# Lightning attention and FNet mixing: the second pair's first layer in two levels, its weight sums moved, folds and output stores reordered

## The chip, the cores and the metric

The kernel runs on one core of a Trainium2 chip. The metric is the device time of one execution in microseconds; lower is better. "Time before" is the median of three runs.

## The reference

Inputs: q, k, v of shape (4, 8, 768, 64), a decay `lam` per head, and two weight matrices of 512 x 2048 and 2048 x 512. All is fp32. The two stages, cut to what matters:

```python
# stage 1: per head, blocks of 64 rows, a running state of 64x64
intra = (qb @ kb.T * Dmask) @ vb
inter = (qb * lam_pow) @ kv_state
out   = intra + inter
kv_state = lam_block * kv_state + (kb * rev_pow).T @ vb
# bridge: (B, H, S, D) -> x of shape (B, S, 512)
# stage 2
mixed = real(fft(fft(x, axis=1), axis=2))
u  = x + mixed
un = (u - mean(u)) / sqrt(var(u) + 1e-6)      # over the last axis
y  = u + maximum(un @ w_ch1, 0) @ w_ch2
```

## The kernel before, in words

TensorE (PE) does all matrix products in fp32; one fp32 matmul leaves two records in the trace. The 24 row tiles of 128 rows (4 batches `b`, 6 tiles each) are grouped in twos: `ORDER` lists 12 groups, the first four are `PLAIN`, the last eight `LATE`. `HC` is 3, `G` is 2, `DM` 512, `DFF` 2048.

*Front, to about 421 us.* `attn(b)` walks six chunks of 128 rows per batch. `fft_ln(b)` does the Fourier mixing: symmetric parts of x are first folded on VectorE (DVE), so that PE multiplies by small cosine and sine matrices. `fold_a(b)` folds the rows that a gather brings mirrored, `fold_b(b, sets)` the rest, for two blocks of 128 and 65 rows, each with an even set `fe` (named `e`) and an odd set `fo` (named `o`). Per block it issues the two full-row folds (L435, L436), the half-row ones (L438, L439), one ScalarE copy, and then even and odd ones in turn (L479 to L493); the second block follows the first. Then PE makes five pieces, `for i in range(5)` (matmul L525); pieces 0, 1 and 4 read the even sets, 2 and 3 the odd ones. A layer norm follows in `norm`. Groups in `PLAIN` go through the plain perceptron `mlp` (first layer L643, second L657, output additions L668 and L669), woven with the attention of the next batch by a list of due times. The normalised rows of `LATE` groups are stored to DRAM as `utd`, their residual rows as `ud`. `combine_weights` (L708) makes Strassen-like sums of weight blocks: `s2.A` and `s2.B` name seven left and right factors, `PRODUCTS` pairs them.

*Late part, 421 us to the end.* The eight `LATE` groups are four pairs j = 0..3 of 512 rows. Both layers of a pair are 2x2 block products done with seven multiplications instead of eight. One level: `first_layer(j)` runs eight column blocks of seven products of width 256 (L892). Two levels: `deep_first(j, k)` splits each of the seven products again into seven, so it has 49 units of four matmuls of width 128 (L977); `deep_second(j, k)` (L1047, reads L1053 and L1055) is the second layer in two levels. `DEEP = 2` gives pairs 0 and 1 the one-level first layer and pairs 2 and 3 the two-level one.

A two-level product needs four sums of the quarters of its weight block, S1 to S4. Three of them are kept in DRAM (`sd`, `td` for the second layer) and loaded again as `tx` tiles by SyncE (SP) one product ahead (`prepare_w`, `prepare_b`, `load_three`); S3 overwrites quarter A21 of its block. GpSimd (POOL) makes the sums of w2 during `first_layer(0)` (`keep_sums`) and those of w1 during `first_layer(1)` (`keep_sums_w`), with SP storing them; `place_sums_w` then loads the seven S3 into place with SP.

`inputs(j)` combines a pair's activations, which `load_u(j)` fetches in two halves of 512 KB into the single `ur` buffer: in the two-level form eight DVE sums (L805 to L822) and ten GpSimd ones (L828 to L832). For the one-level form they are four DVE sums (L793 to L799). `load_u(j + 1)` is issued by SP at the end of `first_layer(j)`, or after product 6 of `deep_first`.

`in_step` fixes the order of the late part: a list of products, each of seven units; product k issues its units at ticks 7k, 7k + 2, up to 7k + 12, so two neighbouring products alternate, and the inputs of product k + 1 are made one step per tick during product k. `seven(mm, read)` goes through seven units on three PSUM banks X, Y, Z; a unit's result is read (L1055 on DVE, L1053 on ScalarE) before the bank takes the next one. After product 1 and 3 of the second layer GpSimd adds the residual rows (`add_u`, L1061); at 5 and 6 the tiles are stored.

`store(b, T, y, cols)` writes a finished tile. Row tiles T < 3 go by a plain DMA on SP (L630); the others have mirrored rows and go by an indirect DMA on GpSimd (L632). Both write into the one tensor `out`. For the last pair, product 5 ends with one store, and product 6 with three.

In `tc.keep_in_program_order` the program's order is kept for an instruction; others may be placed by the scheduler by its own estimates of time. Both orders follow from the code when it is built.

Of the kernel before, what the change touches and what calls it, by code (L numbers as in the profile page):

```python
# [76 lines left out]
def kernel(  # L77
# [25 lines left out]
    G = 2  # L103
# [138 lines left out]

    xs, xn_, xd = {}, {}, {}
# [47 lines left out]
    def attn_out(b, c, head):  # L291
# [23 lines left out]
        if not last:  # L315
            pu = psum_a([128, HP, D])
            for hp in range(HP):
                for hi in range(2):
                    h = 2 * hp + hi
                    mm(pu[HD[hi], hp, :], lhsT=kd[:, h, :], rhs=vt[:, h, :], start=True, stop=True)  # L320
            if c == 0:
                nc.vector.tensor_copy(s_new, pu)
            else:
                nc.gpsimd.tensor_tensor(s_new, s_old, spow.broadcast_to([128, HP, D]), op=ALU.mult)
                nc.vector.tensor_tensor(s_new, s_new, pu, op=ALU.add)
            if not padded:
                yield 0.9
# [39 lines left out]
        if b not in TURNED:  # L367
            x = xn_[b, c] = new(xp, [C, DM], "x") if c < HC else new(xn, [C, DM], "xn")
            back(oT, x)
            if c == 0:  # L370
                xd[b] = (dram.tile([S - 256, DM], F32, name=f"xa{b}"), dram.tile([257, DM], F32, name=f"xb{b}"))
                nc.scalar.dma_start(xd[b][1][256:257], x[0:1])
            elif not last:
                nc.scalar.dma_start(xd[b][0][(c - 1) * C:c * C], x)
            if c >= NC - 2:
                nc.scalar.dma_start(xd[b][1][(c - NC + 2) * C:(c - NC + 3) * C], x)
            if c == NC - 2 and b - 1 not in LEADS:
                mirror_a(b)
            elif last:
                mirror_b(b)  # L380
            yield 1.7
            return
# [85 lines left out]

    def fold_b(b, sets):
# [30 lines left out]
    def fft_ln(b):  # L500
# [19 lines left out]
        for i in range(5):  # L520
# [106 lines left out]

    def store(b, T, y, cols=slice(0, DM)):
        if T < HC:
            nc.sync.dma_start(out[b, 128 * T:128 * T + 128, cols], y[:, cols])  # L630
        else:
            nc.gpsimd.indirect_dma_start(out=out.rearrange("b s d -> (b s) d"),  # L632
                                         out_offset=row_of(2 + HC * (b + 1) + T - HC),
                                         in_=y[:, :], in_offset=None)
# [98 lines left out]
    s2.sd = []  # L733

    def quarters_w(t):

        return [t[:, k, f:f + FH // 2] for f in (0, FH // 2) for k in range(2)]

    def keep_sums_w(k):

        pin = tc.keep_in_program_order
        A11, A12, A21, A22 = quarters_w(s2.A[PRODUCTS[k][0]])
        S3, S2, S1, S4 = [new(s2.yp, [128, FH // 2], "tx", bufs=6) for _ in range(4)]
        s2.sd.append([dram.tile([128, FH // 2], F32, name=f"sd{k}{i}") for i in range(4)])
        for i, o, x, y, op in ((3, S3, A11, A21, SUB), (1, S2, A22, S3, SUB), (0, S1, S2, A11, ADD), (2, S4, A12, S2, SUB)):
            pin(nc.gpsimd.tensor_tensor(o, x, y, op=op))
            nc.sync.dma_start(s2.sd[k][i], o)
# [29 lines left out]
    DEEP = 2  # L777
# [107 lines left out]
    def first_layer(j):  # L885
# [24 lines left out]
        for i in range(HF):  # L910
# [17 lines left out]
            if j < min(DEEP, 2) and i < len(PRODUCTS):  # L928
# [13 lines left out]
        if j + 1 < PAIRS:  # L942
            load_u(j + 1)
# [7 lines left out]
    def seven(mm, read):  # L951

        X, Y, Z = (bank() for _ in range(3))
        for m, ps, start, where in ((0, X, True, (0, 0, 1)), (1, Y, True, (0, 0, 0)), (2, X, False, (1, 0, 1)),
                                    (3, Z, True, (1, 1, 1)), (4, X, False, (1, 1, 0)), (5, Z, False, (1, 0, 0)),
                                    (6, X, False, (0, 1, 1))):
# [7 lines left out]
    def deep_first(j, k):  # L964
# [25 lines left out]

        yield from seven(mm, read)
# [39 lines left out]
    def deep_second(j, k):  # L1031
# [18 lines left out]
        def read(ps, s, m, first):  # L1050
# [3 lines left out]
            else:  # L1054
                V.tensor_tensor(o, ps[:, 0:HM // 2], o, op=ADD)  # L1055

        yield from seven(mm, read)
# [91 lines left out]
    def late():  # L1149
        for j in range(PAIRS):  # L1150
            if j < DEEP:
                open_pair(j)
                if j == 0:
                    run(inputs(0))
                first_layer(j)
                if j + 1 < DEEP:
                    in_step(second_layer(j) + [(inputs(j + 1), iter(()))])
# [116 lines left out]
```

## Time and profile before

| what | value |
|---|---|
| median of 3 runs | 791.47 us (790.59 to 792.36) |
| the profiled execution | 791.45 us |
| its span on the core | 789.2 us |
| mean TensorE clock granted | 0.997 |
| TensorE busy | 761.4 us, 96% |
| VectorE busy | 586.2 us, 74% |
| GpSimd busy | 198.2 us, 25% |

The span runs from the first to the last recorded event; 2.25 us of the execution lie outside it. Busy time adds up an engine's instructions; an engine can be idle because it waits for another, and only the waits on the chain that ends last lengthen the run. Rows of a timeline give start, length, engine, line, operation, tiles written and read, shapes, and in square brackets the idle time before it with what ended that idle time.

### The profile page before, as it was taken

The numbers are of one execution on the slowest core, as the hardware profiler recorded it, in microseconds if no ns is written. First come the engines' busy times: TensorE is split into PE (matmuls) and PEld (weight loads), VectorE is DVE, ScalarE is ACT, GpSimd is POOL, SyncE is SP. The second block draws the span as 40 slices with busy tenths as digits, with TensorE's granted clock in tenths as the row PEclk, the third lists the DMA queues.
The fourth block names the chain that finished last, engine by engine and source line by source line (L and its number), as shares of the span: only waits on it lengthen the run. The fifth ranks groups of instructions, "written<-read, shape, count | busy, mean of one in ns | idle before, by whom it ended". The sixth has DMA issues, their size and how long they took to land.

```text
span 789.2 us, 14621 instructions
## 1 busy us (share of the span) xinstructions
PE 761.4 (96%) x5616; PEld 646.2 (82%) x5616; DVE 586.2 (74%) x1148; ACT 225.4 (29%) x532; POOL 198.2 (25%) x197
## 2 busy tenths in 40 slices
PE   6989989999999999999999999999999999999996
PEld 5767776858675877858846889988999999999996
DVE  5899889685846382345798998669966699758983
ACT  3765443325531221422101221022211342024300
POOL 3223331011102010211004950289105001220021
PEclk9999999999999999999999999999999999999998
DMA  9978723337843147521343375245944455455442
GB/s 230 266 157 226 197 100 121 93 65 208 224 134 87 54 81 146 135 87 41 72 102 107 149 253 151 89 174 200 350 144 148 148 176 185 130 172 186 127 124 79
DMA packets 152331, 116.80 MB, mean 148 GB/s; under 512 B 113998, under 2 KB 113998, under 8 KB 152262
## 3 DMA queue, kind: packets, MB, share of 16 engines
q1 hardware_dynamic: 147120, 103.39, 46.7%
q0 software_dynamic: 2112, 6.69, 2.5%
q10 hardware_dynamic: 3030, 5.78, 2.0%
q8 instruction: 45, 0.74, 0.4%
q14 instruction: 24, 0.20, 0.1%
HBM read 83.58 MB, written 32.25 MB: 147 GB/s over the span
## 4 chain that ended last, share of the span: by engine, by line
PE 82%; DVE 9%; DMA 4%; issue 2%; ACT 2%; POOL 1%; POOLq 0%; ACTq 0%
PE p L1047 22%; PE p L892 12%; PE p L977 11%; PE pm L657 11%; PE pm L643 10%; PE pa L525 3%; PE pa L341 3%; PE pa L300 3%; DMA x<-xb,ix 2%; PE pa L335 2%; PE pa L276 1%; PE pa L320 1%; PE pa L281 1%; PE pa L357 1%; DVE sc L304 1%
## 5 line engine op out<-in xcount | busy, mean ns | idle before, releaser
L643 PE MATMUL pm<-ut,w 128*128 128x256 f32 x512 | 118.4, 381 | 0.0
L657 PE MATMUL pm<-w,hr 128*128 128x512 f32 x256 | 115.3, 596 | 0.1
L643 PEld LDWEIGHTS pm<-ut,w 128*128 128x128 f32 x512 | 94.5, 190 | 13.6 <-issue 2.1
L657 PEld LDWEIGHTS pm<-w,hr 128*128 128x128 f32 x256 | 46.7, 190 | 50.3 <-issue 48.9
L1061 POOL TENSOR_TENSOR y<-y,u 128x512 f32<-128x512 f32 x12 | 18.9, 1571 | 199.1 <-DVE y L1070 156.7
L1047 PE MATMUL p<-tx,sx 128*128 128x128 f32 x416 | 54.9, 275 | 0.0
L1047 PEld LDWEIGHTS p<-tx,sx 128*128 128x128 f32 x416 | 50.6, 192 | 0.0
L892 PE MATMUL p<-ur,w 128*128 128x256 f32 x192 | 46.7, 379 | 0.0
L272 POOL TENSOR_TENSOR kd<-k,decay 128x512 f32<-128x512 f32 x20 | 22.6, 1129 | 95.4 <-PE pa L320 55.9
L1053 ACT COPY y<-p 128x128 f32<-128x128 f32 x48 | 12.8, 267 | 104.1 <-PE p L1047 103.1
L1055 DVE TENSOR_TENSOR y<-p,y 128x128 f32<-128x128 f32 x92 | 25.6, 286 | 22.5 <-PE p L1047 15.9
L892 PEld LDWEIGHTS p<-ur,w 128*128 128x128 f32 x192 | 36.4, 190 | 5.3 <-issue 0.5
L1047 PE MATMUL p<-w,ha 128*128 128x128 f32 x288 | 37.4, 275 | 0.0
L304 DVE TENSOR_TENSOR sc<-pa,decay 128x512 f32<-128x512 f32 x48 | 31.5, 683 | 7.4 <-PE pa L300 7.2
L300 PEld LDWEIGHTS pa<-qT,kT 64*128 64x128 f32 x384 | 26.1, 193 | 12.8 <-ACT qT L283 7.6
L1047 PEld LDWEIGHTS p<-w,ha 128*128 128x128 f32 x288 | 35.0, 192 | 0.2
L651 ACT ACTIVATE hr<-pm 128x256 f32<-128x256 f32 x44 | 16.7, 385 | 62.5 <-PE pm L643 62.2
L300 PE MATMUL pa<-qT,kT 64*128 64x128 f32 x384 | 30.8, 292 | 3.2 <-ACT qT L283 2.9
L892 PE MATMUL p<-sx,w1s 128*128 128x256 f32 x128 | 32.9, 380 | 0.5 <-DVE sx L795 0.5
L558 POOL TENSOR_SCALAR ve<-mv 128x2 f32<-128x2 f32 x12 | 3.3, 279 | 117.6 <-DVE mv L555 117.6
L341 PE MATMUL pa<-sc,v 128*64 128x128 f32 x384 | 30.6, 283 | 2.0 <-DVE sc L304 1.9
L632 POOL DMA_INDIRECT out_dram<-y,ix x12 | 12.7, 1057 | 77.3 <-DVE y L669 56.0
(234 smaller groups left out, 1734.7 us busy)
## 6 DMA issues: line engine op xcount, KB each, us to landing
tx<-td SPq DMA_DIRECT2D x84, 256.0 KB, 2.8
raw<-in_moe_w_ch_dram SPq DMA_DIRECT2D x32, 512.0 KB, 4.4
tx<-sd SPq DMA_DIRECT2D x42, 256.0 KB, 2.7
sd<-tx SPq DMA_DIRECT2D x28, 256.0 KB, 2.0
k<-in_k_dram SPq DMA_DIRECT2D x24, 256.0 KB, 5.9
q<-in_q_dram SPq DMA_DIRECT2D x24, 256.0 KB, 4.3
v<-in_v_dram SPq DMA_DIRECT2D x24, 256.0 KB, 5.1
td<-tx SPq DMA_DIRECT2D x21, 256.0 KB, 2.0
```

Source lines behind the costliest of these rows:

```text
L272: nc.gpsimd.tensor_tensor(kd, kt, kpow, op=ALU.mult)
L300: mm(pss[hi][:, hp, :], lhsT=kT[HD[hi], hp, :], rhs=qT[HD[hi], hp, :], start=True, stop=True)
L304: nc.vector.tensor_tensor(t, pss[hi], decay[:, hi::2, :], op=ALU.mult)
L341: mm(po[HD[hi], hp, :], lhsT=vt[:, 2 * hp + hi, :], rhs=sc[hi][:, hp, :], start=(c == 0 and hp == 0), stop=(hp == HP - 1), skip_group_chec ...
L525: mm = nc.tensor.matmul(ps[:, n, :], lhsT=piece(a, i, n), rhs=cs[0:rows, a, i in (2, 3), n, :], start=(a == 0), stop=(a == 1))
L643: nc.tensor.matmul(ps, lhsT=w1[:, c, 128 * fc:128 * fc + 128], rhs=ut[:, c, :], start=(c == 0), stop=(c == KO - 1))
L657: nc.tensor.matmul(ps, lhsT=hr[(fc - f0) // 4][:, fc % 4, 128 * i:128 * i + 128], rhs=w2[:, fc, :], start=(fc == f0), stop=(fc == f1 - 1))
L892: nc.tensor.matmul(ps, lhsT=s2.A[a][:, kt, 128 * i:128 * i + 128], rhs=U[b][:, kt, :], start=(first and kt == 0), stop=(kt == 1), skip_gro ...
L977: nc.tensor.matmul(ps[:, 128 * i:128 * i + 128], lhsT=ab[m][0][:, 128 * i:128 * i + 128], rhs=ab[m][1], start=(start and i == 0), stop=Tru ...
L1047: nc.tensor.matmul(ps[:, 0:HM // 2], lhsT=ab[m][0][i], rhs=ab[m][1][:, i, :], start=(start and i == 0), stop=(i == HF // 2 - 1), skip_grou ...
L1055: V.tensor_tensor(o, ps[:, 0:HM // 2], o, op=ADD)
L1061: nc.gpsimd.tensor_tensor(o, y, u, op=ADD)
```

## The change

`DEEP` becomes 1: pair 1 takes the two-level first layer too. The sums of w1 are therefore needed before pair 1 begins. They are made in four places:

- `front_sums`: products 0, 1 and 5, on DVE after the state update of chunk 1 of batch 3, into spare front tiles, stored by GpSimd's queue.
- `sums_of_first`: products 3 and 4, on DVE during the second layer of pair 0, one step after every second read of products 2 to 4, staged in a tile that has the place of `ur`, stored by GpSimd's queue.
- `sums_beside(2)` and `sums_beside(6)`: on GpSimd, at product 5 of the second layer of pair 0 and at the first product of pair 1.
- `place_sums_w` loads three S3 instead of seven; in the other four products S3 is made in place.

`load_u(j + 1)` for pair 1 moves from the end of `first_layer(0)` to after product 4 of the second layer of pair 0. Separately, `folds_apart` replaces `fold_b` for b = 2 and 3: the even folds of both blocks are issued first, then the odd ones; and pieces are made in the order 0, 1, 4, 2, 3 for every b. The output is written through two views declared disjoint, one for SP and one for GpSimd. The last pair's product 6 runs its units in the order 0, 2, 3, 5, 4, 1, 6, and part of its tiles are stored at product 5, the last tile in parts. The core of the diff:

```diff
+    def block_sums(eng, queue, k, t, stage, inside, pin=tc.keep_in_program_order):
+        Q11, Q12, Q21, Q22 = quarters_w(t)
+        d = sums_of[k] = [dram.tile([128, DFF // 4], F32, name=f"sd{k}{i}") for i in range(4)]
+        o = dict(enumerate(stage))
+        if inside:
+            o[3] = Q21
+        for i, x, y, op in ((3, Q11, Q21, ALU.subtract), (1, Q22, 3, ALU.subtract), (0, 1, Q11, ALU.add), (2, Q12, 1, ALU.subtract)):
+            x, y = (o[z] if isinstance(z, int) else z for z in (x, y))
+            pin(eng.tensor_tensor(o[i], x, y, op=op))
+            if i < 3 or not inside:
+                queue.dma_start(d[i], o[i])
+            yield 0.0
+
+    def front_sums():
+        fa, fb = slice(0, DFF // 2), slice(DFF // 2, DFF)
+        for k, a in ((0, w1[:, 0:2, fa]), (1, w1[:, 2:4, fa]), (5, w1[:, 2:4, fb])):
+            third = new(fp, [128, DM + 4], "ds")[:, 0:DM]
+            second = new(np_, [128, DM], "un", bufs=1)
+            first_, fourth = (new(ep, [128, DM], "e") for _ in range(2))
+            yield from block_sums(nc.vector, nc.gpsimd, k, a, (first_, second, fourth, third), False, lambda i: i)
...
-                nc.vector.tensor_tensor(s_new, s_new, pu, op=ALU.add)
+                grown = nc.vector.tensor_tensor(s_new, s_new, pu, op=ALU.add)
...
+            if (b, c) == (B - 1, 1):
+                with tc.issue_after(grown.ins):
+                    run(front_sums())
...
+    def folds_apart(b, sets):
+        tt = nc.vector.tensor_tensor
+        parts = [(eo[b][a], xs[b, a][0:n], xs[b, HC + a][0:n], n) for a, n in enumerate(BLK)]
+        for (e, o), lo, hi, n in parts:
+            tc.keep_in_program_order(tt(e[0:n, 0, 0:DM], lo, hi, op=ALU.add))
+            tt(e[0:n, 0, 1:HM], e[0:n, 0, 1:HM], e[0:n, 0, HM:DM - 1], op=ALU.add)
+            nc.scalar.copy(e[0:n, :, HM:HM + 1], e[0:n, :, DM - 1:DM])
...
+        for (e, o), lo, hi, n in parts:
+            tc.keep_in_program_order(tt(o[0:n, 0, 0:DM], lo, hi, op=ALU.subtract))
...
-            run(fold_b(b, sets))
+            run((folds_apart if b > 1 else fold_b)(b, sets))
...
-        for i in range(5):
+        for i in (0, 1, 4, 2, 3):
...
+    out_low, out_high = dram_disjoint_views(out.rearrange("b s d -> (b s) d"), 2)
...
-            nc.sync.dma_start(out[b, 128 * T:128 * T + 128, cols], y[:, cols])
+            row = S * b + 128 * T
+            nc.sync.dma_start(out_low[row:row + 128, cols], y[:, cols])
         else:
-            nc.gpsimd.indirect_dma_start(out=out.rearrange("b s d -> (b s) d"),
+            nc.gpsimd.indirect_dma_start(out=out_high,
...
-        for k, (a, _) in enumerate(PRODUCTS):
-            nc.sync.dma_start(quarters_w(s2.A[a])[2], s2.sd[k][3])
+        for k in (0, 1, 5):
+            tc.keep_in_program_order(nc.sync.dma_start(quarters_w(s2.A[PRODUCTS[k][0]])[2], s2.sd[k][3]))
+
+    def sums_of_first():
+        ur = new(s2.up, [128, 2, KO, G * 128], "ur").rearrange("p a b c -> p (a b c)")
+        for k in (3, 4):
+            yield from block_sums(V, nc.gpsimd, k, s2.A[PRODUCTS[k][0]], four(ur), True)
+
+    def sums_beside(k):
+        u = [new(s2.yp, [128, G, DM], "u2", bufs=2).rearrange("p s c -> p (s c)") for _ in range(2)]
+        run(block_sums(nc.gpsimd, nc.gpsimd, k, s2.A[PRODUCTS[k][0]], four(*u), True))
...
-    DEEP = 2
+    DEEP = 1
...
-                (keep_sums, keep_sums_w)[j](i)
+                keep_sums(i)
...
-        if j + 1 < PAIRS:
-            load_u(j + 1)
         open_y(j)
...
+        if (j, k) == (DEEP, 0):
+            sums_beside(6)
         yield from seven(mm, read)
...
+            P.reads = P.reads + 1
+            if P.sums and P.reads % 7 in (1, 3, 5):
+                next(P.sums, None)
+        if j < DEEP and k == 2:
+            P.sums = sums_of_first()
+        if j < DEEP and k == 5:
+            sums_beside(2)
-        yield from seven(mm, read)
+        yield from seven(mm, read, (0, 2, 3, 5, 4, 1, 6) if (j, k) == (PAIRS - 1, 6) else range(7))
...
+            if j < DEEP:
+                run(P.sums)
+                load_u(j + 1)
         elif k == 5:
             store(*who[1][1], yt[:, 1, 1])
+            if j == PAIRS - 1:
+                store(*who[1][0], yt[:, 1, 0])
+                store(*who[0][0], yt[:, 0, 0], slice(0, HM))
         else:
             store(*who[0][1], yt[:, 0, 1])
-            store(*who[1][0], yt[:, 1, 0])
-            store(*who[0][0], yt[:, 0, 0])
+            if j == PAIRS - 1:
+                for m in (0, HM // 2):
+                    store(*who[0][0], yt[:, 0, 0], slice(HM + m, HM + m + HM // 2))
```

More of the change, by code (lines that the diff above doesn't have):

```diff
@@ L7 @@
 from concourse import mybir
+from concourse.bass_types import dram_disjoint_views
 from concourse.masks import make_identity
@@ L240, in weights, with quarters_w @@
                 yield 1.0
+    def quarters_w(t):
+        return [t[:, k, f:f + DFF // 4] for f in (0, DFF // 4) for k in range(2)]
+    sums_of = {}
+    def block_sums(eng, queue, k, t, stage, inside, pin=tc.keep_in_program_order):
[17 more added lines that the diff above has]
+            yield from block_sums(nc.vector, nc.gpsimd, k, a, (first_, second, fourth, third), False, lambda i: i)
     xs, xn_, xd = {}, {}, {}
@@ L467, in fold_a @@
             yield from fold_x(b, a, n, 1, eo[b][a][1][0:n, 1, 0:DM], xn_[b, HC + a][0:n])
+    def folds_apart(b, sets):
[5 more added lines that the diff above has]
+            nc.scalar.copy(e[0:n, :, HM:HM + 1], e[0:n, :, DM - 1:DM])
+            am = e[0:n, :, W:2 * W]
+            lo, hi = e[0:n, 0, 0:HM + 1], e[0:n, 1, 0:HM + 1]
+            tt(am[:, 0, 0:HM + 1], lo, hi, op=ALU.add)
+            tt(am[:, 1, 0:HM + 1], lo, hi, op=ALU.subtract)
+            lo, hi = am[:, :, 0:QM], am[:, :, HM:QM:-1]
+            tt(e[0:n, :, 0:QM], lo, hi, op=ALU.add)
+            tt(e[0:n, :, QM:HM], lo, hi, op=ALU.subtract)
+            yield 2.4
+        for (e, o), lo, hi, n in parts:
+            tc.keep_in_program_order(tt(o[0:n, 0, 0:DM], lo, hi, op=ALU.subtract))
+            tt(o[0:n, 0, 1:HM], o[0:n, 0, 1:HM], o[0:n, 0, HM:DM - 1], op=ALU.subtract)
+            bm = o[0:n, :, W:2 * W]
+            lo, hi = o[0:n, 0, 1:HM], o[0:n, 1, 1:HM]
+            tt(bm[:, 0, 1:HM], lo, hi, op=ALU.subtract)
+            tt(bm[:, 1, 1:HM], lo, hi, op=ALU.add)
+            lo, hi = bm[:, :, 1:QM + 1], bm[:, :, HM - 1:QM - 1:-1]
+            tt(o[0:n, :, 0:QM], lo, hi, op=ALU.subtract)
+            tt(o[0:n, :, QM:HM], lo, hi, op=ALU.add)
+            yield 2.4
+            sets.append((e, o))
+        eo.pop(b)
     def fold_b(b, sets):
@@ L731, in keep_sums, with four @@
             nc.sync.dma_start(s2.td[k][i], o)
[L733 to L747, printed above, removed]
-    def place_sums_w():
-        for k, (a, _) in enumerate(PRODUCTS):
-            nc.sync.dma_start(quarters_w(s2.A[a])[2], s2.sd[k][3])
+    s2.sd = sums_of
+    def four(*tiles):
+        return [t[:, i:i + 512] for t in tiles for i in range(0, t.shape[1], 512)]
+    def place_sums_w():
+        for k in (0, 1, 5):
[7 more added lines that the diff above has]
+        run(block_sums(nc.gpsimd, nc.gpsimd, k, s2.A[PRODUCTS[k][0]], four(*u), True))
     def load_u(j, queue=nc.sync):
@@ L927, in first_layer @@
             last = (i, X, Z)
-            if j < min(DEEP, 2) and i < len(PRODUCTS):
+            if i < len(PRODUCTS):
                 if i == 0:
                     tc.keep_in_program_order(nc.gpsimd.tensor_copy(s2.begun, h["a11"][:, 0, 0, 0:1]))
-                (keep_sums, keep_sums_w)[j](i)
+                keep_sums(i)
             if i == HF - 3:
@@ L949, in part_sum, with seven @@
             e.tensor_tensor(o[:, s], x[:, s], y[:, s], op=op)
-    def seven(mm, read):
+    def seven(mm, read, order=range(7)):
         X, Y, Z = (bank() for _ in range(3))
-        for m, ps, start, where in ((0, X, True, (0, 0, 1)), (1, Y, True, (0, 0, 0)), (2, X, False, (1, 0, 1)),
-                                    (3, Z, True, (1, 1, 1)), (4, X, False, (1, 1, 0)), (5, Z, False, (1, 0, 0)),
-                                    (6, X, False, (0, 1, 1))):
+        steps = ((0, X, True, (0, 0, 1)), (1, Y, True, (0, 0, 0)), (2, X, False, (1, 0, 1)),
+                 (3, Z, True, (1, 1, 1)), (4, X, False, (1, 1, 0)), (5, Z, False, (1, 0, 0)),
+                 (6, X, False, (0, 1, 1)))
+        for m, ps, start, where in (steps[i] for i in order):
             if m:
@@ L1055, in read @@
                 V.tensor_tensor(o, ps[:, 0:HM // 2], o, op=ADD)
-        yield from seven(mm, read)
+            P.reads = P.reads + 1
+            if P.sums and P.reads % 7 in (1, 3, 5):
+                next(P.sums, None)
+        if k == 0:
+            P.reads, P.sums = 0, None
+        if j < DEEP and k == 2:
[3 more added lines that the diff above has]
+        yield from seven(mm, read, (0, 2, 3, 5, 4, 1, 6) if (j, k) == (PAIRS - 1, 6) else range(7))
         def add_u(o, y, k, m):
@@ L1086, in deep_second @@
             V.tensor_tensor(y12, y12, T, op=ADD)
+            if j < DEEP:
+                run(P.sums)
+                load_u(j + 1)
         elif k == 5:
             store(*who[1][1], yt[:, 1, 1])
+            if j == PAIRS - 1:
+                store(*who[1][0], yt[:, 1, 0])
+                store(*who[0][0], yt[:, 0, 0], slice(0, HM))
         else:
             store(*who[0][1], yt[:, 0, 1])
-            store(*who[1][0], yt[:, 1, 0])
-            store(*who[0][0], yt[:, 0, 0])
+            if j == PAIRS - 1:
+                for m in (0, HM // 2):
+                    store(*who[0][0], yt[:, 0, 0], slice(HM + m, HM + m + HM // 2))
+            else:
+                store(*who[1][0], yt[:, 1, 0])
+                store(*who[0][0], yt[:, 0, 0])
     def sum_s3(j):
@@ L1149, in late @@
     def late():
[L1150 to L1157, printed above, removed]
+        open_pair(0)
+        run(inputs(0))
+        first_layer(0)
         in_step(second_layer(DEEP - 1) + [w for j in range(DEEP, PAIRS) for w in deep_pair(j)])
```

## The prediction

> **What bounds the kernel now.** I read the page first, then busy time by windows, then the chain of waits, then timelines where the diff bites.
>
> ```profile
> PE 761.4 (96%) x5616; PEld 646.2 (82%) x5616; DVE 586.2 (74%) x1148; ACT 225.4 (29%) x532; POOL 198.2 (25%) x197
> ```
>
> TensorE bounds the span of 789.2 us; 28 us are not its own. The windows (stretch, length, then busy time of each engine) say where:
>
> ```profile
> 262.00:345.00 83.00, 83.00 (x631) 63.87 (x631) 36.71 (x82) 22.30 (x57) 12.70 (x17) 1.00 0.45 102
> 421.00:607.00 186.00, 185.46 (x1240) 173.24 (x1239) 155.87 (x278) 33.15 (x97) 91.93 (x73) 1.00 0.52 176
> 607.00:782.00 175.00, 174.68 (x1565) 174.49 (x1563) 138.71 (x247) 45.61 (x95) 26.28 (x30) 1.00 0.49 151
> ```
>
> From 421 us PE idles under 1 us, so PE work removed there is time gained, and work on VectorE, GpSimd or a queue is free until it makes PE wait. The chain of waits (start, length, what) is PE alone at the end, and closes with an output store:
>
> ```profile
> 696.82 38.41 PE p L977 x344
> 740.59 35.75 PE p L1047 x320
> 776.93 4.39 DMA out_dram<-y,ix
> ```
>
> **The second pair's first layer.** From the PE timeline, one-level and two-level rows:
>
> ```profile
> 553.96 1.03 PE L892 MATMUL p<-sx,w1s 128*128 128x256 f32 x4
> 554.83 1.89 PE L892 MATMUL p<-ur,w 128*128 128x256 f32 x8
> ...
> 610.89 1.06 PE L977 MATMUL p<-sx,tx 128*128 128x128 f32 x8
> 611.79 1.06 PE L977 MATMUL p<-sx,w1s 128*128 128x128 f32 x8
> ```
>
> Matmul ends overlap, so I take start to start. One-level: four records (one product of width 256) in 0.87 and 1.72/2 = 0.86; I use 0.864. Two-level: eight records in about 0.893 (the last units of the run begin at 777.05, 777.95, 778.84 and 779.73, the same spacing). The first layer of pair 1 has 8 blocks × 7 = 56 units, 56 × 0.864 = 48.4 us; afterwards 7 × 7 = 49 units, 49 × 0.893 = 43.8 us. **−4.6 us**, firm, as the other two pairs already run this form in a dense window.
>
> **Early folds (b = 2 and 3).** The PE timeline has one wait in each, for an even fold (L484) of the second block:
>
> ```profile
> 256.04 1.25 PE L525 MATMUL pa<-cs,fe 65*128 65x193 f32 x6 [1.75 <-DVE fe L484]
> ...
> 366.09 1.09 PE L525 MATMUL pa<-cs,fe 65*128 65x193 f32 x5 [0.95 <-DVE fe L484]
> ```
>
> VectorE starts the first block when a gather has landed and alternates even and odd:
>
> ```profile
> 247.97 0.69 DVE L435 TENSOR_TENSOR fe<-x,x 128x512 f32<-128x512 f32 x1 [2.83 <-DMA x<-xb,ix]
> 248.58 0.69 DVE L436 TENSOR_TENSOR fo<-x,x 128x512 f32<-128x512 f32 x1
> ```
>
> The steps are 0.61 for a whole-row operation and 0.34 for a half. Both blocks' evens are 2 × (0.61 + 5 × 0.34) = 4.6 us, so evens end near 252.6, plus about 1 us for a ScalarE copy between two of them: 253.6–254.0, before PE asks at 254.3. Gain 1.75. For b = 3 VectorE can start at 357.8: evens end near 363.0, while in the changed order of PE's instructions the first even piece stands where PE would come at about 362.5. A rest of about 0.5 may stay: gain 0.45. The odd folds end 257–259 and 366–368, and PE, which takes piece 4 ahead of 2 and 3, wants them at about 261 and 369. The changed order of pieces for b = 0 and 1 only permutes PE work: 0 ± 0.2. Does the gain reach the end? Between 345 and 421 VectorE combines weights; it then has 2.0 us idle before L668 at 421.5, which waits on PE, so an earlier PE finds a VectorE that can be about 2 us earlier. **−2.2 us** (−1.0 to −2.7).
>
> **The block sums' new places.** GpSimd lost 28 sums in the pair-1 first layer (PE dense beside them: worth 0). In their stead:
>
> - 12 VectorE sums of 128x512 at 301.7–319 (12 × 0.61 = 7.3 us). VectorE is idle there for 8.33, 3.03, 3.03 and 3.43 us ahead of the reads at 310.0, 313.5, 316.9 and 321.4; PE is at 100%. Every read has at least one spare PSUM buffer. The 12 GpSimd stores at about 1.0 us each (nearest row: L632, 1057 ns mean) hold back one state decay needed at 324 and the kd products at 319.4. Value 0, bounds 0 and +1.5.
> - 8 VectorE sums at 480–500, one at every second read, beside about 6 us of idle time: 4.9 us, lag at most 1.3. PE reaccumulates a bank four units later (3.6 us, 2.7 after the unit itself), so nothing shows: 0.
> - SP's loads `place_sums_w` fall from 7 to 3, its 28 stores go: 0, as SP gated nothing there.
>
> **The reload of `ur`.** This is the new wait. The last of the eight sums leaves VectorE near 497.8; its GpSimd store lands near 501.1; only then may SP issue the two halves of `ur` (all staged in it), which take 5.7 us (the page's issue rows: `ur<-utd` 5.7). SP keeps its queue order, so a `td` load and half 1 stand behind the first half: half 1 lands near 507.6. VectorE's first operation on it is due at 506.8 (the same operation of the next pair, L805, 598.96, minus the 92.2 us period). So it is 0.8 to 1.7 us late. Before, SP issued this load at 470.5, and it cost nothing.
>
> At the same time GpSimd makes four sums and three stores (504–512) beside eight SBUF-to-SBUF operations of VectorE, and it shows what that costs:
>
> ```profile
> 501.70 1.33 DVE L873 TENSOR_TENSOR sx<-sx,ha 128x512 f32<-128x512 f32 x1
> ...
> 503.73 0.99 DVE L875 TENSOR_TENSOR sx<-ha,sx 128x512 f32<-128x512 f32 x1 [0.30 <-PE p L1047]
> 504.64 0.28 DVE L1055 TENSOR_TENSOR y<-p,y 128x128 f32<-128x128 f32 x1
> 504.84 0.68 DVE L793 TENSOR_TENSOR sx<-ur 128x512 f32<-128x512 f32 x1
> ```
>
> Beside a GpSimd operation of 1.27 us the same shape takes 1.33 or 0.99 instead of 0.68: +0.65 or +0.31. Four meetings at up to 0.65 are 2.6 us. The Trainium skill (page "SBUF — State Buffer", section "SBUF: two separate sides") goes further: VectorE with two SBUF inputs and a GpSimd operation that reads SBUF take one port pair as an exclusive lock, and the loser waits for the whole instruction. By that rule a meeting may cost up to 1.27 us, four of them 5.1. The row decides: nothing here lost more than about one GpSimd operation's half, so I take 2.6. Lag 1.3 + 2.6 = 3.9 us; PE feels what exceeds 2.7: **+1.2 us** by the row, +3.7 by the rule. Lower bound 0 (meetings missed), upper bound +4.
>
> The same page warns, in its box on VectorE blocking DMAs, that a GpSimd-queue DMA starves while VectorE runs a two-port mode, which speaks against storing by GpSimd. It names copies and single-input operations, not two-input sums; the indirect stores here land in 2.7–2.9 us beside a busy VectorE, so I charge nothing.
>
> **The tail.** The end of the old run: PE's last unit starts 780.63, VectorE's last read is at 781.72, GpSimd issues an indirect store at 782.09, and SP's two stores come 3 us later, because both write `out` and SP waits for the indirect landing:
>
> ```profile
> 782.09 0.97 POOL L632 DMA_INDIRECT out_dram<-y,ix  x1 [4.16 <-DVE y L1055]
> 784.91 0.81 SPq L630 DMA_DIRECT2D out_dram<-y  x2
> ...
> SPq L630 <- DMA out_dram<-y,ix: 14.4, 2, 10.9
> ```
>
> (the last line is of the waits of SP). The span closes at 789.2. Two views remove that wait, and half of the last pair's output leaves at product 5. What is late next: the indirect store of `who[0][1]`. It is ready near 780.2 but stands behind the previous indirect store (issued 776.93, 4.39 us, so 781.3): issue 781.4, landing 784.2–785.8. SP's two last pieces issue at 782.1–782.5 and land near 784.7. Add the 1.2 us that lay between last landing (788.0) and end: 786.0–787.0, **−2.8 us** (−1.5 to −3.4).
>
> **The sum.** −4.6 −2.2 −2.8 +1.2 = −8.4. The profiled execution took 791.45 (span 789.2 and 2.25 around it), 0.02 from the median 791.47. 791.45 − 8.4 = **783.1 us**, span about 780.8.
>
> **Rivals.**
> - *No new stall* (0.22): GpSimd's sums fall between VectorE's operations and `ur` is on time. −9.6: 781.9; with the best fold and tail bounds 780.3.
> - *Smaller gains, larger stall* (0.20): tail −1.5, folds −1.0, stall +2 to +3.7: −5.1 to −3.4, so 786.3–788.1. The indirect landing of 4.39 us speaks for the tail part; the page's lock rule for the stall.
> - *The `ur` chain becomes the bound* (0.07, slower or no gain): sum, GpSimd store, SP reload, VectorE and PE in series, with SP's queue in order behind the wait. Hidden while half 1 lands by about 509; after that each microsecond is one of PE. To cancel the 9.6 us gained it must land near 519–520, i.e. a GpSimd store must be 11 us late. For it: GpSimd's queue stands ahead of SP's, and a wait there delays three more things. Against: the six stores stand ahead of GpSimd's three long additions at 500, and stores land in under 3 us. At 13 us late: about 793.
> - *It does not do what it says*: excluded for the order of instructions. In the built program SP's last stores wait on no GpSimd DMA, and even folds stand first.
>
> **How the numbers follow.** My forecast (783.1) has 0.51, the rivals 0.22, 0.20 and 0.07. Measurement tells apart about 0.2% (1.6 us). The range 780.3 to 787.5 takes in the forecast, the first rival and most of the second. Slower by over 0.2% gets 0.05, within it 0.03, faster 0.92.
>
> **What would show it.** Right: PE's first-layer stretch of pair 1 is 43.8 us of L977-like units; no PE gap before the even pieces of b = 2, under 0.6 for b = 3; SP's last stores no longer wait on an indirect landing; PE gaps of about 1 us in total near 505–515. Wrong: PE gaps over 4 us behind the `ur` reload, SP's `ur` issue after 505, fold gaps unchanged, or the last indirect store landing after 786.

## The result, and the profile after

| | before | after |
|---|---|---|
| median | 790.92 us (14 executions) | 787.33 us (14 executions) |
| ratio | | 0.9949, interval 0.993 to 0.9969 |
| profiled execution | 791.45 us, span 789.2 | 784.18 us, span 782.3 |

The kernel became faster by 4.0 us by the ratio (0.51% of 791) and by 3.6 by the medians, where 8.4 were forecast; 787.33 lies just inside the range given. Two later sets of executions of the unaltered changed kernel had ratios of 0.994 (0.9917 to 0.9962) and 0.9931 (0.9904 to 0.9957). Over all sets, executions of either kernel spread over 8 us and more. Two traces of the changed kernel, 8 us apart, differ almost only ahead of 130 us, where little of the change lies (the order of the fold pieces of b = 0). So below I compare stretches that begin there.

The marks are lines of the chain of waits (start, length, what): the first fold product of b = 1 (the expectations below call it that of b = 0), the start of the long first-layer stretch of pair 0 on the chain, and the last long second-layer stretch. Before (the third mark, 740.59, is in the prediction):

```profile
130.96 2.63 PE pa L525 x16
...
423.72 45.13 PE p L892 x208
```

After:

```profile
129.91 2.62 PE pa L588 x16
...
421.64 45.15 PE p L959 x208
...
736.35 41.11 PE p L1115 x368
```

| stretch | before | after | difference |
|---|---|---|---|
| front (first mark to second) | 292.76 | 291.73 | −1.03 |
| late (second to third) | 316.87 | 314.71 | −2.16 |
| tail (third to end of span) | 48.61 | 45.95 | −2.66 |
| sum | 658.24 | 652.39 | −5.85 |

Another 1.05 us of the two profiled spans' difference lies before the first mark, and 0.37 outside the span (2.25 before, 1.88 after). Each column is one trace. In later traces of the same code the front and the late stretch differ from these by up to 0.5 us, so smaller differences say nothing.

TensorE is still the bound (first part of the page), and the windows show where it has gaps now (same columns as in the prediction):

```profile
PE 756.1 (97%) x5784; PEld 646.6 (83%) x5784; DVE 603.0 (77%) x1159; ACT 231.9 (30%) x532; POOL 190.5 (24%) x210
```

```profile
262.00:345.00 83.00, 82.15 (x630) 61.75 (x630) 46.41 (x93) 21.34 (x56) 19.99 (x30) 1.00 0.55 144
421.00:607.00 186.00, 183.53 (x1437) 177.40 (x1437) 160.57 (x276) 40.82 (x99) 82.44 (x80) 1.00 0.56 184
607.00:775.00 168.00, 168.00 (x1507) 168.00 (x1506) 136.70 (x241) 44.19 (x93) 22.29 (x24) 1.00 0.50 151
```

The first window had 83.00 of 83.00 before, the second 185.46 of 186.00. The PE timeline names the gaps; the wait for b = 2 (1.75 us) is gone, that for b = 3 is not, and three are new (one of 0.94 at 147 us is the same in both kernels):

```profile
312.86 4.15 PE L709 MATMUL pm<-ut,w 128*128 128x256 f32 x18 [0.85 <-DVE hr L715]
...
361.52 1.25 PE L588 MATMUL pa<-cs,fe 65*128 65x193 f32 x6 [0.97 <-DVE fe L515]
...
508.60 1.16 PE L1115 MATMUL p<-w2s,sx 128*128 128x128 f32 x8 [0.72 <-DVE y L1123]
...
512.75 1.16 PE L1115 MATMUL p<-tx,sx 128*128 128x128 f32 x8 [1.21 <-DVE y L1123]
```

All are waits for VectorE. At 508 to 513 its timeline shows both suspects at once, operations that last two to three times 0.68 us and a wait for the reload of `ur`:

```profile
502.91 1.42 DVE L1162 TENSOR_TENSOR y<-y 128x512 f32<-128x512 f32 x1
504.25 0.28 DVE L1123 TENSOR_TENSOR y<-p,y 128x128 f32<-128x128 f32 x1
504.45 1.56 DVE L1163 TENSOR_TENSOR y<-y,t 128x512 f32<-128x512 f32 x1
506.12 0.29 DVE L1123 TENSOR_TENSOR y<-p,y 128x128 f32<-128x128 f32 x1
507.65 0.69 DVE L872 TENSOR_TENSOR ur<-ur 128x512 f32<-128x512 f32 x1 [1.24 <-DMA ur<-utd]
508.26 0.28 DVE L1123 TENSOR_TENSOR y<-p,y 128x128 f32<-128x128 f32 x1
508.46 1.88 DVE L875 TENSOR_TENSOR sx<-ur 128x512 f32<-128x512 f32 x1
...
510.47 1.23 DVE L877 TENSOR_TENSOR ur<-ur 128x512 f32<-128x512 f32 x1
```

What the two PE waits cost is read from starts: neighbouring units begin 0.89 us apart, but the two that waited begin 1.78 and 2.26 after their predecessors and each is followed by one gap of 1.00. That is 0.89 + 1.37 + 0.11 + 0.11, about 2.47 us, more than the 1.93 in brackets. (A unit is the eight records of one two-level product.)

The front sums held VectorE too. Behind its waits for the staging tiles' stores stands a read that TensorE needs:

```profile
304.05 0.69 DVE L259 TENSOR_TENSOR ds<-w 128x512 f32<-128x512 f32 x1 [4.18 <-DMA sd<-ds]
...
310.33 0.69 DVE L259 TENSOR_TENSOR e<-w,un 128x512 f32<-128x512 f32 x1 [3.04 <-DMA sd<-e]
311.06 0.69 DVE L259 TENSOR_TENSOR un<-w,ds 128x512 f32<-128x512 f32 x1
311.78 0.69 DVE L259 TENSOR_TENSOR ds<-w 128x512 f32<-128x512 f32 x1
312.39 0.42 DVE L715 TENSOR_SCALAR hr<-pm 128x256 f32<-128x256 f32 x1
```

In the tail SP's stores now wait for VectorE and no longer for an indirect store (waits of SP from 760 us to the end: total, times, longest):

```profile
SPq L696 <- DVE y L1123: 10.8, 3, 8.0
```

### The profile page after: what moved, and what is told of

Its sections match the earlier page's. It is cut to its first block, busy times and chain, and to the rows that moved or that the text cites. A ratio compares the mean times of both kernels' runs of the same rounds, so it can differ in the third digit from the quotient of the medians.

```text
span 782.3 us, 14993 instructions
## 1 busy us (share of the span) xinstructions
PE 756.1 (97%) x5784; PEld 646.6 (83%) x5784; DVE 603.0 (77%) x1159; ACT 231.9 (30%) x532; POOL 190.5 (24%) x210
## 4 chain that ended last, share of the span: by engine, by line
PE 80%; DVE 10%; DMA 4%; issue 3%; ACT 2%; POOL 1%; SPq 0%; DVEq 0%; POOLq 0%; ACTq 0%
PE p L1115 21%; PE p L1043 17%; PE pm L723 11%; PE pm L709 10%; PE p L959 6%; PE pa L588 3%; PE pa L330 3%; PE pa L371 3%; DMA x<-xb,ix 2%; PE pa L365 1%; PE pa L306 1%; PE pa L350 1%; DVE sc L334 1%; PE pa L311 1%; PE pa L387 1%
## 5 line engine op out<-in xcount | busy, mean ns | idle before, releaser
L1115 PE MATMUL p<-tx,sx 128*128 128x128 f32 x400 | 52.8, 275 | 1.2 <-DVE y L1123 1.2
L1115 PEld LDWEIGHTS p<-tx,sx 128*128 128x128 f32 x400 | 48.6, 192 | 1.4 <-DVE y L1123 1.4
L1052 DVE TENSOR_TENSOR ha<-p,ha 128x512 f32<-128x512 f32 x60 | 40.1, 685 | 10.0 <-PE p L1043 9.8
L1052 DVE TENSOR_TENSOR hs<-p,hs 128x512 f32<-128x512 f32 x39 | 26.2, 684 | 14.1 <-PE p L1043 14.1
L1043 PE MATMUL p<-sx,tx 128*128 128x128 f32 x264 | 33.9, 275 | 0.0
L1043 PEld LDWEIGHTS p<-sx,tx 128*128 128x128 f32 x264 | 31.6, 192 | 0.0
```

Source lines behind the costliest of these rows:

```text
L1043: nc.tensor.matmul(ps[:, 128 * i:128 * i + 128], lhsT=ab[m][0][:, 128 * i:128 * i + 128], rhs=ab[m][1], start=(start and i == 0), stop=Tru ...
L1052: V.tensor_tensor(o, p, o, op=ADD)
L1115: nc.tensor.matmul(ps[:, 0:HM // 2], lhsT=ab[m][0][i], rhs=ab[m][1][:, i, :], start=(start and i == 0), stop=(i == HF // 2 - 1), skip_grou ...
```

## The experiments

Three things were open: whether the changed kernel is uneven in itself, why 2.47 us are lost at 508 to 513, and where the rest of the folds' gain went. Stretches are front / late / tail as in the table, in us. The code cuts are cut to what matters.

**The changed kernel again (twice), unaltered.**

> The changed kernel once more, unaltered. Its first executions fell between 784.1 and 793.7 us, those of the kernel before between 789.5 and 794.8. If the changed kernel itself is uneven (it waits on something that is not always equally late), the new executions spread over 784 to 794 again, median about 787, and some are near 784.3. If the spread came from the chip of the first runs, they now lie within 2 us of each other.

Measured: median 787.13 us (before 791.76), 785.28 to 792.4. The profiled execution took 792.4, and its excess is all at the start. The windows of the first profile and then of this one, 20 to 35 us:

```profile
20.00:25.00 5.00, 4.16 (x60) 3.32 (x57) 4.87 (x11) 4.23 (x9) 0.30 (x1) 1.00 1.10 279
25.00:30.00 5.00, 4.10 (x43) 3.68 (x44) 4.93 (x9) 3.40 (x10) 1.43 (x2) 1.00 1.05 249
30.00:35.00 5.00, 5.00 (x66) 3.95 (x63) 4.22 (x9) 2.74 (x8) 2.29 (x2) 1.00 1.04 292
```

```profile
20.00:25.00 5.00, 4.03 (x58) 3.12 (x56) 2.82 (x5) 2.29 (x6) 0.62 (x1) 1.00 0.90 227
25.00:30.00 5.00, 1.54 (x12) 1.30 (x14) 4.09 (x8) 2.31 (x4) 1.06 (x1) 0.80 0.79 177
30.00:35.00 5.00, 5.00 (x30) 4.34 (x28) 3.71 (x7) 3.62 (x10) 0.67 (x1) 0.52 0.93 229
```

In order of time: from 20 to 25 us the DMA engines moved 227 instead of 279 GB/s, while the granted clock was still 1.00; then TensorE was busy for 1.54 us of 5.00; and the clock granted was 0.80 and then 0.52. So in this trace the slower loads stand ahead of the lower clock. That the one brought on the other, and why the loads were slower, is not shown. The first mark falls at 137.70 instead of 129.91; the stretches behind it are 292.16 / 314.71 / 45.93, within 0.5 us of the first profile. So the opening varies, not the changed parts; theories A and B of the expectations below look for the spread in those, and these traces speak against both.

> The changed kernel unaltered for the third time, to narrow the median: the stretches behind the opening say 5.9 us less than before plus 0.4 outside the span; the medians of the first two sets said 4.0 and 4.6, of executions whose opening (before 130 us) differs by up to 8 us. If the opening is only chance, this set may lie anywhere between 3.5 and 7 under the kernel before; if the changed kernel has the later opening, near 4 again. In the trace, front, late stretch and tail are 291.7 to 292.2, 314.7 and 45.9.

Measured: median 785.57 (before 790.74), 5.2 us less; stretches 291.94 / 315.22 / 45.91. The three sets of the changed kernel lie 3.6, 4.6 and 5.2 us under before by their medians. The stretches of its three traces say 5.2 to 5.9, and 0.4 more outside the span. The opening varies by enough to make up the difference; whether the changed kernel opens later on the average, or by chance in these sets, was not shown.

**Folds and tail without the two-level first layer.** The sums are made where they were before: `keep_sums_w` is back, and `front_sums`, `sums_of_first` and `sums_beside` are gone with their calls.

```diff
--- after
-            if (b, c) == (B - 1, 1):
-                with tc.issue_after(grown.ins):
-                    run(front_sums())
...
-    DEEP = 1
+    DEEP = 2
...
```

> The kernel before, with the even folds first, the order 0, 1, 4, 2, 3, the two views and the divided last tile; the second pair keeps its one-level first layer and its sums on GpSimd. All theories: 2.1 us from the folds and 2.6 us from the tail, so about 786.5 (before at 791.2). On the spread they differ. Theory A, the new sums in the front make VectorE wait for stores that are unevenly late: without them the executions lie within 2 us. Theory B, the chain of sum, store and reload of ur is unevenly late: the same, within 2 us. Theory C, a denser TensorE is granted less clock in some executions: they spread over 8 us here too, with granted clocks down to 0.991.

Measured: median 788.1 (before 791.76; ratio 0.9947, 0.993 to 0.9964), 290.90 / 316.87 / 46.61. The late stretch is that of before to 0.01 us. The front fell by 1.86 us, 0.83 more than in the first profile of the changed kernel (1.0 and 1.3 more than in its later two): that is what the front sums cost. Executions lay between 786.7 and 790.2: theory C did not show here.

**The two views alone.**

```diff
--- before
+    out_low, out_high = dram_disjoint_views(out.rearrange("b s d -> (b s) d"), 2)
...
-            nc.sync.dma_start(out[b, 128 * T:128 * T + 128, cols], y[:, cols])
+            row = S * b + 128 * T
+            nc.sync.dma_start(out_low[row:row + 128, cols], y[:, cols])
...
-            nc.gpsimd.indirect_dma_start(out=out.rearrange("b s d -> (b s) d"),
+            nc.gpsimd.indirect_dma_start(out=out_high,
...
```

> The kernel before with the two disjoint views of the output and nothing else. If the wait of SP's last stores for an indirect store's landing was the cost of the tail, the time from TensorE's last long stretch to the end falls from 48.61 to about 46.2 us (2.4 less; the changed kernel has 45.95, a kernel with the folds and the whole new tail 46.61), and the order of units and the stores in parts add under 0.3. If the size of the last stores counts, it falls by about 1.5 only, and the rest is due to the parts. Median about 789.

Measured: median 789.23 (before 791.36; ratio 0.9969, 0.9958 to 0.998), tail 45.88. The last two issues in its timeline, with VectorE's last read between them, are:

```profile
781.13 0.97 POOL L636 DMA_INDIRECT out_dram<-y,ix  x1 [3.47 <-DVE y L1059]
781.46 0.29 DVE L1059 TENSOR_TENSOR y<-p,y 128x128 f32<-128x128 f32 x1 [0.60 <-PE p L1051]
781.77 0.34 SPq L634 DMA_DIRECT2D out_dram<-y  x1
```

SP issues at 781.77, 0.02 us after the last read ends (781.46 + 0.29), where it issued at 784.91 before. The views alone take 2.73 us, as much as the whole new tail (2.66): the order of units and the stores in parts added nothing that shows. The kernels with the whole new tail lie between 45.27 and 46.61.

**GpSimd's sums later.**

```diff
--- after
-        if (j, k) == (DEEP, 0):
-            sums_beside(6)
+        if j == DEEP and k in (0, 2):
+            sums_beside(2 if k == 0 else 6)
...
-        if j < DEEP and k == 5:
-            sums_beside(2)
```

> The changed kernel with GpSimd's two blocks of sums each moved later: that of product 2 from the second layer of pair 0 (product 5) to the first product of pair 1, that of product 6 from there to the third product of pair 1. If GpSimd's sums beside VectorE's input sums cost the TensorE waits of 0.72 and 1.21 us at 508 to 513 us, both go and the fastest executions come to about 782.3. If the late reload of ur alone makes them, they stay, 784.2. Theory A: the executions spread as those of the changed kernel do. Theory B, if it is these sums that are unevenly slow: they lie within 2 us.

Measured: median 786.27 (before 791.76), 291.86 / 314.68 / 45.89. The wait is there all the same, but now VectorE's operations have their usual length and it waits for the reload (VectorE, then PE):

```profile
511.46 0.69 DVE L872 TENSOR_TENSOR ur<-ur 128x512 f32<-128x512 f32 x1 [3.69 <-DMA ur<-utd]
```

```profile
512.41 1.16 PE L1115 MATMUL p<-w2s,sx 128*128 128x128 f32 x8 [1.56 <-DVE y L1123]
```

In this execution, whose late part begins 3.0 us later than that of the first profile, SP issued the second half at 505.04 and VectorE could start at 511.46. So the reload alone is enough for a stall, and GpSimd's sums are not needed for one. Of the 2.4 us that this late stretch fell short of the 4.63 to be had, about 1.8 lie here and the rest at 555 to 561.

**VectorE's sums and the reload earlier.**

```diff
--- after
-        if j < DEEP and k == 2:
+        if j < DEEP and k == 1:
             P.sums = sums_of_first()
...
             add_u(y22, y22, 1, 1)
+            if j < DEEP:
+                run(P.sums)
+                load_u(j + 1)
         elif k == 4:
...
-            if j < DEEP:
-                run(P.sums)
-                load_u(j + 1)
```

> The changed kernel with VectorE's eight sums of products 3 and 4 begun one product of the second layer earlier, and the reload of ur issued after product 3 instead of product 4; GpSimd's sums stay where they are. The first runs showed that executions differ by up to 8 us before 130 us, in work that no kernel here changes, so I read stretches of the trace: from the first first-layer product of pair 0 to TensorE's long second-layer stretch of pair 3 it is 316.87 us before and 314.71 in the changed kernel, where 4.63 less was to be had; 2.47 is lost at 507 to 513. Theory U, the late reload of ur makes that loss: it lands near 501 now, VectorE does not wait for it, the loss falls to 0.7 or less and the stretch to about 313. Theory L, GpSimd's four sums make it, as VectorE's operations there took 1.2 to 1.9 us instead of 0.68: the loss stays 1.5 to 2.5, the stretch 313.7 or more.

Measured: median 785.67 (before 791.36; ratio 0.9926, 0.9903 to 0.9949), 291.79 / 314.97 / 45.87. SP issues the two halves at 497.81 and 498.65, VectorE no longer waits for them, and yet the stall is as large, with long operations in VectorE's row (VectorE, GpSimd, then PE):

```profile
506.21 1.85 DVE L872 TENSOR_TENSOR ur<-ur 128x512 f32<-128x512 f32 x1
507.98 0.28 DVE L1123 TENSOR_TENSOR y<-p,y 128x128 f32<-128x128 f32 x1
508.18 2.04 DVE L875 TENSOR_TENSOR sx<-ur 128x512 f32<-128x512 f32 x1
```

```profile
506.20 1.29 POOL L259 TENSOR_TENSOR u<-u,w 128x512 f32<-128x512 f32 x1
...
508.37 1.29 POOL L259 TENSOR_TENSOR u<-w,u 128x512 f32<-128x512 f32 x1
```

```profile
512.63 1.16 PE L1115 MATMUL p<-tx,sx 128*128 128x128 f32 x8 [1.38 <-DVE y L1123]
```

Beyond 0.68 each, the five slowed operations (1.42, 1.55, 1.85, 2.04, 1.23) lost 4.69 us while GpSimd made its four sums (4.4 of it by these sums: the last operation, which meets another GpSimd operation, still takes 0.97 without them in the kernel without GpSimd sums below). The late stretch lost 2.73 us with the sums alone, 2.47 with both. Theory U falls as the only cause, theory L as well: each is sufficient, so taking one away leaves the other.

**Three edits at once** (the two above, and the front staging below).

> The changed kernel with three edits at once: front staging tiles as in the kernel before this one, VectorE's late sums and the reload of ur one product earlier, and GpSimd's two blocks of sums one and two products later. If the losses found are all there are: front stretch 290.9, late stretch 312.3, tail as in the changed kernel: 9.1 us under the kernel before in the trace, about 782 median. If what is taken away at one place returns at the next (moving GpSimd's blocks alone lost 0.6 us at 557): 783 to 785.

Measured: median 784.62 (before 791.36; ratio 0.9903, 0.9881 to 0.9926), 291.98 / 313.75 / 45.90. The waits at 508 to 513 are gone, but GpSimd's moved sums meet VectorE's two-input sums 20 us on, where two operations take 4.28 us, and a PE wait appears (VectorE, then PE):

```profile
530.31 4.28 DVE L1067 TENSOR_TENSOR hs<-hs,ha 128x512 f32<-128x512 f32 x2
```

```profile
535.25 1.16 PE L1043 MATMUL p<-sx,tx 128*128 128x128 f32 x8 [0.80 <-DVE hs L1052]
```

So the late stretch kept 1.51 us of loss: "returns at the next place" was right.

**No GpSimd sums in the late part.** The same sums on VectorE, one after a read, with the early reload:

```diff
--- sums and reload earlier
-        run(block_sums(nc.gpsimd, nc.gpsimd, k, s2.A[PRODUCTS[k][0]], four(*u), True))
+        return block_sums(V, nc.gpsimd, k, s2.A[PRODUCTS[k][0]], four(*u), True)
...
+        if j == DEEP and k in (0, 2):
+            P.more = sums_beside(2 if k == 0 else 6)
...
+            if k in (0, 2) and P.more:
+                next(P.more, None)
...
```

(The last two lines stand in `read()`; the other calls of `sums_beside` are gone.)

> As the kernel with the sums and the reload one product earlier, and the sums of products 2 and 6, which GpSimd made, are made by VectorE instead, one after each read of the first and the third two-level product of pair 1 (their three stores each stay on GpSimd's queue). So no GpSimd sum meets VectorE's two-input operations at 502 to 513 or at 517 to 533. If port sharing is the rest of the loss (VectorE's operations took up to 2.2 us instead of 0.68 beside GpSimd's sums), the late stretch falls to 312.3 to 312.6 us (before 316.87, changed kernel 314.71, the kernel with all three edits 313.75), and the median to about 783. If VectorE has no room for 8 more sums (8 times 0.61 = 4.9 us in 14 products' units), TensorE waits there instead, and the stretch stays at 313.5 to 315.

Measured: median 783.85 (before 790.75; ratio 0.9919, 0.9887 to 0.995), 291.78 / 312.48 / 46.24. No PE wait is left in the late part, and the late stretch is 4.39 us under before, where 4.63 were to be had. The same two operations as above, with GpSimd silent:

```profile
505.81 0.69 DVE L872 TENSOR_TENSOR ur<-ur 128x512 f32<-128x512 f32 x1
506.42 0.28 DVE L1127 TENSOR_TENSOR y<-p,y 128x128 f32<-128x128 f32 x1
506.62 0.68 DVE L875 TENSOR_TENSOR sx<-ur 128x512 f32<-128x512 f32 x1
```

This shows the sharing: 1.85 and 2.04 us with GpSimd's sums, 0.69 and 0.68 without.

**The front sums' stores on SP.**

```diff
--- after
-            yield from block_sums(nc.vector, nc.gpsimd, k, a, ...
+            yield from block_sums(nc.vector, nc.sync, k, a, ...
```

> The changed kernel with the twelve stores of the front sums issued by SP instead of GpSimd. Theory A, VectorE waits up to 4.2 us for GpSimd's stores of the staging tiles, with reads of PSUM behind it: SP's stores land in about 2 us (td<-tx: 2.0), the waits in VectorE's row at 300 to 318 us fall under 2 us, the TensorE wait of 0.85 us at 312 goes, fastest executions 783.3, and the executions lie within 3 us. Theories B and C: the spread stays 8 us. It may cost if SP's loads of k, q and v stand behind stores that wait for VectorE: then up to 2 us more.

Measured: median 788.42 (before 791.76), 293.91 / 315.22 / 45.27. The forecast missed: the wait at 312 went, but the front grew by 2.2 us, and the executions spread over 8 us where 3 were expected. SP's row has the sums' stores between the loads of k, q and v, and holds one pair of them for 7.45 us; the waits for even folds of b = 3 were 1.68 and 0.55. TensorE's order changed in this stage as well, so the two are not told apart.

**More staging for the front sums.**

```diff
--- after
-            first_, fourth = (new(ep, [128, DM], "e") for _ in range(2))
+            first_, fourth = (new(xp, [128, DM], "x") for _ in range(2))
```

> The changed kernel with two of the four staging tiles of each front block taken from the x pool instead of the two e tiles. Theory: VectorE's waits of 4.2, 3.0 and 0.6 us for stores come from too few staging tiles, and the TensorE wait of 0.85 us at 312 from the read that stands behind one of them. Then the 3.0 us wait and the TensorE wait go, and the stretch from the first fold matmul of b = 0 to the first first-layer product falls from 291.73 to about 290.9, what the kernel without front sums shows (290.90). Rival: stores issued by GpSimd's queue are slow here in themselves, and the wait only moves to the next store: 291.7 stays. The order of TensorE's instructions changes a little in this stage too: plus or minus 0.5.

Measured: median 786.56 (before 791.36), 291.83 / 314.71 / 46.22. The rival was right in effect: the wait at 312 goes, the stretch stays. So that wait was not what the front sums cost, or something of the same size took its place. The first wait of VectorE for a store remained (4.21 us), and the scheduler put nine of the twelve sums after 316 us, among the attention of the next chunk, where a PE wait of 0.53 (for ScalarE) appeared at 329. What makes up the 0.8 us is therefore open.

**The old fold order for b = 3.**

```diff
--- after
-            run((folds_apart if b > 1 else fold_b)(b, sets))
+            run((folds_apart if b == 2 else fold_b)(b, sets))
```

> The changed kernel with the even folds first for b = 2 only; b = 3 has the old order. Theory: for b = 3 the new order gained nothing, because TensorE's order was moved with it (five groups of first-layer products now stand behind the fold pieces and not ahead of them): the wait for an even fold at about 361 to 366 is 0.95 again in place of 0.97 to 1.11, and the stretch from the first fold matmul of b = 0 to the first first-layer product stays at 291.7 to 292.2. Rival: it had gained 0.5 or more, hidden in other waits; then the stretch grows to 292.2 or more with a wait of 1.5.

Measured (one execution, 785.13 us): 291.86 / 314.69 / 45.89, and the wait is there in the same size:

```profile
364.99 2.24 PE L588 MATMUL pa<-cs,fe 65*128 65x193 f32 x12 [0.96 <-DVE fe L547]
```

It comes 3.5 us later (361.52 before this edit), because first-layer products stand ahead of it. The new order had gained nothing for b = 3.

**A version that goes further.** As the kernel without GpSimd sums in the late part, and:

```diff
-            yield 12.0 if b - 1 in LEADS else 9.0
+            yield 12.0 if b - 1 in LEADS else (9.0 if b == 2 else 12.0)
```

> As the kernel without GpSimd sums in the late part (late stretch 312.48 us), and for b = 3 the due time behind the folds is 12.0 instead of 9.0, which puts eight first-layer matmuls ahead of the first fold piece on TensorE instead of between and behind the pieces. If TensorE's wait of 1.11 us at 362 is only a matter of that order, it goes: the front stretch falls from 291.78 to about 290.7, the sum from the first fold matmul to the end from 650.5 to 649.4, median about 782.5. Rival: the pieces' results come later and a wait of the same size appears at the layer norm or at the first product at 422: front stretch 291.8 again.

Measured: median 783.49 (before 790.74; ratio 0.9906, 0.9877 to 0.9935), 291.17 / 312.46 / 46.19, sum 649.82: 8.4 us under before, 2.6 under the changed kernel. Beside it the changed kernel had a median of 785.57; with six executions each, the intervals of the two ratios overlap, so that it is the faster of the two rests on the stretches. The wait for the even fold is gone, but 0.46 us came back ahead of the last second-layer stretch of the plain perceptron, so the gain is 0.6 and not 1.1:

```profile
391.25 27.73 PE L723 MATMUL pm<-w,hr 128*128 128x512 f32 x64 [0.46 <-DVE hr L715]
```

## Why the prediction was right, and where its sizes were off

The direction, the parts and the places were right; the forecast gain of 8.4 us was too large by 2.55 against the stretches of the trace, and by more against the medians. Of the 2.55 the stall is 1.27, the front sums 0.83, the folds 0.34 and the tail 0.14 (the last two within what traces of one kernel differ by). That 787.33 fell inside the range, by less than 0.2 us, was partly luck: the opening alone moves an execution by 8.

- *First layer, −4.6 us.* Right. Between the second-layer marks a one-level pair takes 92.18 us in the trace of before (563.49 − 471.31) and a two-level one 87.55 (740.59 − 653.04): 4.63. In the kernel without GpSimd sums, where nothing stalls, 4.39 of it came out.
- *The transition, +1.2 us.* The mechanism was right, the term was mis-sized: 2.47. The failed step is "Beside a GpSimd operation of 1.27 us the same shape takes 1.33 or 0.99 instead of 0.68: +0.65 or +0.31. Four meetings at up to 0.65 are 2.6 us." It took two rows for the price of a meeting. GpSimd's rows of before beside them show what they measure:

```profile
501.22 1.27 POOL L1061 TENSOR_TENSOR t<-t,u 128x512 f32<-128x512 f32 x1
502.44 1.72 POOL L1061 TENSOR_TENSOR y<-y,u 128x512 f32<-128x512 f32 x1
```

  VectorE began at 501.70 and 503.73, when 0.79 and 0.43 us of these additions were left, and ended 0.54 to 0.56 us behind their ends. It paid the rest of an addition that was well under way. The new sums it meets at their start: with the early reload, GpSimd's sums end at 507.49 and 509.66, and VectorE's operations, begun at 506.21 and 508.18, at 508.06 and 510.22, again 0.56 or 0.57 behind. In the late parts of six traces (before, after, and the four kernels that move these sums or the reload one by one, together, or to VectorE), each of the 114 two-input SBUF operations of 512 columns that took over 0.78 us ended 0.54 to 0.59 us behind a GpSimd operation. So a meeting costs what is left of the GpSimd operation: 0.74, 0.87, 1.17 and 1.36 us with the early reload, 4.1 us for the four sums (4.4 by the comparison with the kernel without them). The Trainium skill's rule of an exclusive lock (page "SBUF — State Buffer", section "SBUF: two separate sides"), with its 5.1 us for four meetings, agrees with the trace far better than the 2.6. Its sum for the stall, +3.7, was too high all the same: in the changed kernel the third sum met nothing, since VectorE was waiting for `ur` then.
- *What TensorE does not feel, 2.7 us.* Mis-sized too. VectorE lost 1.24 us to the reload and 0.74, 0.88, 1.20 and 0.55 to GpSimd (the rows above less 0.68), 4.6 in all, where 3.9 were reckoned. TensorE lost 2.47, so about 2.1 were absorbed by this estimate, and 2.0 with the early reload (4.69 against 2.73).
- *The reload, "0.8 to 1.7 us late".* VectorE's wait for it was 1.24 us in the first profile, 1.76 in the third set's, and 3.69 with GpSimd's sums out of the way, when VectorE came to it sooner. The hit was partly luck: the last sum left VectorE at 495.40 and not 497.8, and its store held SP until 500.67, so that landing took about 2 us longer than the 3.3 reckoned.
- *Folds, −2.2 us.* −1.75 for b = 2 was right. The 0.45 for b = 3 was not: the even fold that TensorE waits for ended 5.7 us after the gather (355.75 to 361.47) and the last of them 6.1, where 5.2 were put, since two reads of `hr` fell between, and TensorE's order put the pieces forward. I had the moved order in the sum, but not the reads.
- *Front sums, 0.* Cost 0.83, inside the bounds 0 to 1.5. "VectorE is idle there" was true; but a sum that waits 3 to 4 us for a store holds back the read behind it, as the rows at 310 to 312 show. I had counted VectorE's busy time only, and "stores land in under 3 us" did not hold: those of `un` on GpSimd's queue had a median of 5.0. As the wait at 312 could be taken away without gain, how the 0.83 comes about is not shown in full, and how to avoid it was not found.
- *Tail, −2.8 us.* 2.66; all of it from the views.
- *Sum.* −4.63 + 2.47 − 1.86 + 0.83 − 2.66 = −5.85. Of the rivals "smaller gains, larger stall" came nearest (786.3 to 788.1 us): its stall and, with the front sums taken off, its folds fit, its tail of −1.5 does not. The `ur` chain stalled TensorE as described, but far from its price. The lower end of "no new stall" was mis-added: its best bounds make −10.7, which is 780.75 and not 780.3.

## What to carry to other kernels

A stage with idle VectorE time is not free for work on GpSimd or for work that waits: count for each added operation what it locks, for how long, and what stands behind it in order. A row that shows two engines meeting gives the price of that meeting only: look when each of the two began. When a stall has two suspects, take both away, since each alone may sustain it. If two stores go to one tensor but write different rows, declare the parts disjoint: here that alone was worth as much as the whole rebuilt tail.

## What the runs showed of the hardware

Two-input VectorE operations of 128x512 within SBUF, 0.68 us alone, took up to 2.04 us beside single GpSimd sums of 1.3 us; each slowed one ended 0.54 to 0.59 us behind a GpSimd operation, so it had waited for the whole rest of it. VectorE's reads of PSUM with one SBUF input stayed at 0.28 us beside the same sums. In the front VectorE waited 3.04 and 4.18 us for 256 KB stores on GpSimd's queue; what made these slow was not shown. In one trace whose opening took 8 us longer, the loads were slower first and the granted clock fell after that.
